# Lead-in of a fused attention and MLP kernel: one fp32 key load moved from GpSimd's queue to SyncE's, early queries first, and the last key maximum and its block scores put earlier

## The chip, the cores and the metric

One NeuronCore of one Trainium2 chip runs the whole program. The metric is device time in microseconds, as the median of several executions. TensorE (PE), VectorE (DVE), ScalarE (ACT), GpSimd (POOL) and SyncE (SP) each run their own instructions in order and wait for one another through semaphores. DMAs are started by SyncE and GpSimd, each with its own queue.

## What is computed

Inputs are q, k and v of shape (4, 8, 768, 64) and two weight matrices, 512 x 2048 and 2048 x 512, all fp32; the output is 3072 x 512 fp32. Cut to what matters:

```python
block, window = 32, 16
scale = 1.0 / np.sqrt(D)
k_sum = k.reshape(B, H, nb, block, D).max(axis=3)        # one key per block of 32: its maximum
v_sum = v.reshape(B, H, nb, block, D).mean(axis=3)
scores_l = where(|i - j| < window, scale * q @ k.T, -1e9)  # a band of near keys
scores_s = scale * q @ k_sum.T + np.log(block)             # 24 block keys
a = softmax(concat([scores_l, scores_s]))
x = a @ concat([v, v_sum])            # attention, then heads side by side
h = x @ w_in
out = (h * sigmoid(1.702 * h)) @ w_out
```

## The kernel before

Work is in bf16 and fp16 with fp32 accumulation. The four batches go one after another; the attention of the next batch is laid into the MLP of the present one, so that TensorE hardly ever stops. Only the attention of batch 0, first half (384 queries, 8 heads taken as 4 pairs of heads), has nothing to hide behind. That is the lead-in, and all of the change is in it. Weights and the rest of the inputs stream in behind it.

The order of the lead-in is written out by hand: every engine handle is a wrapper (`_Ordered`) that keeps the program order, so the list of calls in the kernel's body is the order on each engine. p counts the pairs of heads, 0 to 3.

- **Loads.** `load_k0_first` brings the fp32 keys of pair 0 by SyncE's queue to the tile k0f and `cast_k0` makes bf16 of them on ScalarE. `load_k0(p)` brings the keys of pairs 1, 2 and 3 by GpSimd's queue, which converts to bf16 on the way (tile kb). `load_q0(g)` brings the early queries of pairs 2g and 2g + 1 the same way (tile qe), `load_v0(p)` the values (tile v0n). Behind them in GpSimd's queue stand the five pieces of w_in, then w_out, late queries, w_out, the masks that GpSimd computes, and the next batch. GpSimd's DMAs use eight semaphores in turn, so each one waits for the landing of the one eight before it.
- **Keys and queries.** `k_turn(p)` transposes a pair's keys on TensorE (12 transposes into a PSUM tile ps_k), `k_own(p, engine)` copies the result to the tile qT (its second buffer). `k_max(p)` takes the maximum of each block of 32 keys on VectorE (tile ks). `q_turn(p)` and `q_copy(p, dve)` do the same for queries (PSUM tile ps_q, first buffer of qT).
- **Scores.** `s_bias(p)` writes the band's bias into PSUM (ps_s), `s_own(p)` and `s_edges(p)` add the scores, `s_exp(p)` takes the exponential on ScalarE (a_sb). `b_turn(g)` computes the block scores of two pairs into ps_b from `k_max`'s result, `b_exp(g)` their exponential (ab).
- **Values.** `v_sum` adds the value blocks on TensorE (ps_vt), `v_copy` copies them (vs). `av_own`, `av_edges` and `av_blocks` make the attention output (ps_av), `v_norm` divides it on VectorE (reciprocal rc, product x). `x_turn` and `x_copy` transpose it for the MLP (ps_x, xT), whose first matmuls (`ff_first`, then `ff_in`, PSUM tile ph) follow. The second MLP matrix goes to po.
- **Fillers.** `idle(n)` issues n matmuls on the tile warm, whose results (ps_h) nobody reads.
- **PSUM.** The lead-in's small PSUM tiles rotate through a pool of four (pturn); s_bias and the last two av_own through a pool of two (pbig).

The profile gives one line, L28 (the wrapper), to all these instructions, so steps are told apart by their tiles.

Of the kernel before, what the change touches and what calls it, by code (L numbers as in the profile page):

```python
# [9 lines left out]
F32 = mybir.dt.float32  # L10
BF16 = mybir.dt.bfloat16
# [3 lines left out]
ACT = mybir.ActivationFunctionType  # L15
# [20 lines left out]
def kernel(  # L36
# [10 lines left out]
    B, H, S, D = q.shape  # L47
# [18 lines left out]
    act = _Ordered(tc, nc.scalar)  # L66
    pool = _Ordered(tc, nc.gpsimd)
    sp = _Ordered(tc, nc.sync)
# [3 lines left out]
    castp2 = ctx.enter_context(tc.tile_pool(name="cast2", bufs=2))  # L72
# [7 lines left out]
    lead = early.enter_context(tc.tile_pool(name="lead", bufs=1))  # L80
    kb2, qb2 = {}, {}

    RK = S // 128
    RQ = 4
    PQ = HALF // RQ
    k0f = lead.tile([128, 2, RK, D], F32, name="k0f")
    qe = lead.tile([PQ, H, RQ, D], BF16, name="qe")

    def k0_rows(p):
        return k[0, 2 * p:2 * p + 2].rearrange("h (p r) d -> p h (r d)", r=RK)  # L90

    def load_k0_first():
        sp.dma_start(out=k0f.rearrange("p h r d -> p h (r d)"), in_=k0_rows(0))

    def cast_k0():
        kb2[0] = castp2.tile([128, 4, RK, D], BF16, name="kb", tag="kb")
        act.activation(out=kb2[0][:, 0:2], in_=k0f, func=ACT.Copy)

    def load_k0(p):
        if p == 2:  # L100
            kb2[1] = castp2.tile([128, 4, RK, D], BF16, name="kb", tag="kb")
        o = 2 * (p % 2)
        pool.dma_start(out=kb2[p // 2][:, o:o + 2].rearrange("p h r d -> p h (r d)"), in_=k0_rows(p))

    def load_q0(g):
        pool.dma_start(out=qe[:, 4 * g:4 * g + 4].rearrange("p h r d -> p h (r d)"),
                       in_=q[0, 4 * g:4 * g + 4, 0:HALF].rearrange("h (p r) d -> p h (r d)", r=RQ))
# [40 lines left out]
    def identity():  # L148
        pool.affine_select(out=ident, in_=ident, compare_op=ALU.not_equal, fill=1.0,
                           base=0, pattern=[[-1, 128]], channel_multiplier=1)  # L150
# [65 lines left out]
    gTb = keep.tile([128, NT, S], F16, name="gT")  # L216
# [48 lines left out]
    def copy(eng, out, in_):  # L265
        if eng is act:
            act.activation(out=out, in_=in_, func=ACT.Copy)
        elif eng == "dve_alone":

            dve.tensor_reduce(out=out, in_=in_.unsqueeze(len(in_.shape)), axis=AX.X, op=ALU.max)  # L270
        else:
            eng.tensor_copy(out=out, in_=in_)
# [21 lines left out]
    def idle(n, cols=128):  # L294

        for i in range(n):
            pe.matmul(out=st["H", 0][:, 0:cols], lhsT=warm[:, 0:128], rhs=warm[:, 0:cols],
                      start=True, stop=True)
# [70 lines left out]
    def turn_plain(ps, src):  # L369

        n, rows = src.shape[0], src.shape[2]
        for r in range(rows):
            for h in range(2):
                pe.transpose(out=ps[h * 64:h * 64 + 64, r * n:r * n + n], in_=src[:, h, r],
                             identity=ident[0:n, 0:n])
# [6 lines left out]
    def k_own(p, eng):  # L382
        copy(eng, kn[:, p].rearrange("p (c r) -> p c r", r=RK),
             st["K", p][:, 0:S].rearrange("p (r c) -> p c r", r=RK))

    def k_max(p):
        dve.tensor_reduce(out=ks0[:, p, 0:nb], in_=kn[:, p].rearrange("p (n s) -> p n s", s=block),
                          axis=AX.X, op=ALU.max)
# [8 lines left out]
    def q_turn(p):  # L397
        if p % 2 == 0:
            st["Q2"] = pturn.tile([128, 1024], BF16, name="ps_q", tag="turn")
        st["Q", p] = st["Q2"][:, p % 2 * HALF:p % 2 * HALF + HALF]  # L400
        turn_plain(st["Q", p], qe[:, 2 * p:2 * p + 2])

    def q_copy(p, eng):
        copy(eng, qT[p][0][:, 0:HALF].rearrange("p (c r) -> p c r", r=RQ),
             st["Q", p].rearrange("p (r c) -> p c r", r=RQ))
# [16 lines left out]
    def s_bias(p):  # L422

        big = st["S", p] = pbig.tile([128, 1024], F32, name="ps_s", tag="big")
        for h in range(2):
            pe.matmul(out=big[:, h * 512:h * 512 + NE], lhsT=ident, rhs=bias, start=True, stop=False,
                      skip_group_check=True)

    def s_own(p):

        big = st["S", p]
        for j in range(JH):
            for h in range(2):
                r, o = slice(h * 64, h * 64 + 64), slice(j * 128, j * 128 + 128)
                pe.matmul(out=big[:, h * 512 + j * 128:h * 512 + j * 128 + 128], lhsT=kn[r, p, o],
                          rhs=qTs[0][r, p, o], start=False, stop=True, skip_group_check=True)

    def s_edges(p):

        big = st["S", p]  # L440
        for j in range(JH):
            for h in range(2):
                r, o = slice(h * 64, h * 64 + 64), h * 512 + HALF + j * 32
                pe.matmul(out=big[0:32, o:o + 32], lhsT=kn[r, p, j * 128 + 128:j * 128 + 160],
                          rhs=qTs[0][r, p, j * 128 + 96:j * 128 + 128], start=False, stop=True,
                          skip_group_check=True)
                if j:
                    pe.matmul(out=big[96:128, o:o + 32], lhsT=kn[r, p, j * 128 - 32:j * 128],
                              rhs=qTs[0][r, p, j * 128:j * 128 + 32], start=False, stop=True,
                              skip_group_check=True)  # L450

    def s_exp(p):
        a = a_sb[p] = lead.tile([128, 2, NE], BF16, name="a_sb", tag="a_sb", bufs=4)
        act.activation(out=a, in_=st["S", p].rearrange("p (h c) -> p h c", h=2)[:, :, 0:NE],
                       func=ACT.Exp, scale=scale)

    def b_turn(g):

        st["B", g] = pturn.tile([128, 512], F32, name="ps_b", tag="turn")
        for i in range(2):  # L460
            for h in range(2):
                o = i * 64 + h * 32
                r = slice(h * 64, h * 64 + 64)
                pe.matmul(out=st["B", g][o:o + 32, 0:HALF], lhsT=ks0[r, 2 * g + i],
                          rhs=qT[2 * g + i][0][r, 0:HALF], start=True, stop=True, skip_group_check=True)

    def b_exp(g):
        ab = st["ab", g] = lead.tile([128, HALF], BF16, name="ab", tag="ab", bufs=2)
        act.activation(out=ab, in_=st["B", g][:, 0:HALF], func=ACT.Exp, scale=scale)
# [9 lines left out]
    def v_sum(ps_):  # L479

        for p in ps_:
            if p == 0:
                t = pturn.tile([128, 512], F32, name="ps_vt", tag="turn")
                st["VT", 0], st["VT", 1] = t[:, 0:2 * D], t[:, 2 * D:4 * D]
                st["VT", 0, 1] = t[:, 0:4 * D]
            elif p > 1:
                st["VT", p] = pturn.tile([128, 512], F32, name="ps_vt", tag="turn")[:, 0:2 * D]
            for i in range(2):
                for j in range(NJ):
                    o = EX - (p % 2 * 2 + i) * 32 - 4 * j  # L490
                    pe.matmul(out=st["VT", p][:, i * D:(i + 1) * D], lhsT=E[:, o:o + 128],
                              rhs=v0n[:, 2 * p + i, j, 0:D],
                              start=(j == 0), stop=(j == NJ - 1), skip_group_check=True)

    def v_copy(ps_, eng):
        h0, n = 2 * ps_[0], 2 * len(ps_)
        copy(eng, vs4[:, h0:h0 + n, 0:D], st[("VT",) + ps_].rearrange("p (h d) -> p h d", d=D))
# [383 lines left out]
    def exp_soon():  # L881
        act.activation(out=gate[:, 1:2], in_=gate[:, 0:1], func=ACT.Exp)


    dve.memset(warm, 0.0)
    dve.memset(wide, 0.0)
    load_k0_first()
    exp_soon()
    cast_k0()
    load_k0(1)  # L890
    identity()
    load_q0(0)
    load_k0(2)
    load_k0(3)
    load_q0(1)
# [24 lines left out]
    idle(4)  # L920
    k_turn(1)
    k_own(1, act)
    k_max(0)
    s_bias(1)
    idle(4)
    q_turn(0)
    q_turn(1)
    q_copy(0, dve)
    q_copy(1, dve)
    idle(8)  # L930
    s_own(0)
    s_own(1)
# [13 lines left out]
    q_copy(2, dve)  # L946
    q_copy(3, dve)
    k_max(2)
    s_bias(2)
    s_bias(3)  # L950
    v_sum((0,))
    s_own(2)
    s_own(3)
    s_edges(2)
    s_exp(2)
    s_edges(3)
    v_sum((1,))
    v_copy((0, 1), dve)
    k_max(3)
    s_exp(3)  # L960
    av_own(0)
    av_own(1)
    av_edges(0)
# [2 lines left out]
    av_blocks(1)  # L966
    v_norm(0)
    v_norm(1)
    b_turn(1)
    v_sum((2,))  # L970
    b_exp(1)
    v_copy((2,), act)
    av_own(2)
    av_edges(2)
# [29 lines left out]
    for e in range(2):  # L1004
        r = slice(64 * e, 64 * e + 64)
        dve.tensor_copy(out=w50[r, JH - e:NJ, e, :, 0:D],
                        in_=v0n[r, :, JH - e:NJ, 0:D].rearrange("p h j d -> p j h d"))
# [104 lines left out]
    for b in range(1, B - 1):  # L1112
        nxt = b + 1 < B
        s = (b + 1) % 2
# [129 lines left out]
```

## Time and profile before

| | |
|---|---|
| median of three executions | 206.87 us (206.80 to 209.70) |
| the profiled execution | 206.51 us, of which the span of the profile is 204.8 us |
| outside the span | 1.7 us |
| TensorE busy | 198.1 us, 97% of the span |
| VectorE, ScalarE, GpSimd busy | 69%, 61%, 45% of the span |
| granted TensorE clock | 0.998 over the span |
| DMA | 27.93 MB, 136 GB/s in the mean |

A busy share is no measure of what bounds the kernel. Three views answer that: the chain of waits (followed back from the last instruction to what released it), the timeline of a stretch, and the DMA issues with their time to landing. Times in them are microseconds from the span's start. A timeline row gives start, duration, engine, line, operation, output and inputs, shape and count, and in brackets the idle time before it with what ended it; DMA rows of POOL and SPq are the issuing of a DMA, not its transfer.

### The profile page before, as it was taken

To read this page: it belongs to the slowest core of one execution; us is meant where nothing else is said; L and a number is where in the kernel's file an instruction comes from. 1 tells how busy PE (TensorE), PEld (TensorE's weight loads), DVE (VectorE), ACT (ScalarE), POOL (GpSimd) and SP (SyncE) were. 2 spreads that over 40 slices of the span, in tenths; PEclk is the share of its full clock that TensorE was granted. 3 is DMA by queue.
4 is the path that set the end of the run, shared out by engine and by line. 5 is a ranking of instruction groups with operands and counts; after the bars stand their busy time and mean duration, and the time that the engine had idled before them with its cause. 6 is when DMAs were issued, how large, how long until landed. Compare 5 with 4: busy or idle time off the path is not lost.

```text
span 204.8 us, 5857 instructions
## 1 busy us (share of the span) xinstructions
PE 198.1 (97%) x2364; PEld 137.4 (67%) x2364; DVE 140.4 (69%) x388; ACT 124.6 (61%) x238; POOL 92.7 (45%) x144
## 2 busy tenths in 40 slices
PE   6989999999999999999999999999999999999992
PEld 6667654556754566665888975657888865578881
DVE  6767894594856874897768689896759546658211
ACT  4385876638786717777871546778661467983220
POOL 7965389555999584002965035000000019990000
PEclk9999999999999999999999999999999999999999
DMA  5999999999999999999999989996023730000222
GB/s 117 153 159 202 207 211 213 195 156 232 134 143 151 177 176 168 159 175 132 123 196 127 154 151 142 122 261 137 0 106 90 160 111 3 0 0 3 102 102 104
DMA packets 95851, 27.93 MB, mean 136 GB/s; under 512 B 83649, under 2 KB 92881, under 8 KB 95825
## 3 DMA queue, kind: packets, MB, share of 16 engines
q0 software_dynamic: 69920, 13.44, 85.2%
q1 hardware_dynamic: 25904, 14.13, 33.2%
q8 instruction: 18, 0.29, 0.6%
q14 instruction: 9, 0.07, 0.1%
HBM read 27.26 MB, written 6.29 MB: 164 GB/s over the span
## 4 chain that ended last, share of the span: by engine, by line
PE 90%; DMA 4%; POOL 2%; DVE 1%; issue 1%; ACT 0%; POOLq 0%; DVEq 0%
PE ph L28 33%; PE poA L28 16%; PE po L28 11%; PE poB L28 7%; PE ps_av L28 4%; DMA v0n<-in_v_dram 4%; PE poC L28 4%; PE phA L28 4%; PE ps_s L28 3%; PE ps_t L28 1%; PE ps_x L28 1%; POOL kb L28 1%; PE phB L28 1%; PE phC L28 1%; PE phE L28 1%; PE ps_vs L28 1%
## 5 line engine op out<-in xcount | busy, mean ns | idle before, releaser
L28 PE MATMUL ph<-xT,w_in_sb 128*128 128x384 f16 x416 | 70.2, 326 | 0.1
L28 PEld LDWEIGHTS <-w_in_sb 128*128 128x128 f16 x452 | 43.7, 98 | 27.8 <-issue 0.2
L28 ACT ACTIVATE gT<-ph 128x384 f16<-128x384 f32 x104 | 49.9, 492 | 18.5 <-PE ph L28 18.1
L28 PEld LDWEIGHTS <-gT 128*128 128x128 f16 x312 | 28.8, 98 | 11.3 <-issue 0.2
L28 ACT ACTIVATE a_sb<-ps_s 128x768 bf16<-128x768 f32 (+1 forms) x32 | 25.0, 826 | 12.5 <-PE ps_s L28 12.5
L28 POOL DMA_DIRECT2D vw<-in_v_dram x36 | 24.6, 700 | 12.4 <-DMA kb<-in_k_dram 4.8
L28 PEld LDWEIGHTS <-gs 128*128 128x128 f16 x288 | 27.7, 98 | 3.4
L28 POOL TENSOR_TENSOR gs<-gT 128x384 f16<-128x384 f16 x9 | 8.2, 911 | 42.3 <-ACT gT L28 42.3
L28 PE MATMUL po<-w_out_sb,gT 128*128 128x512 f16 x96 | 23.6, 380 | 0.0
L28 DVE TENSOR_TENSOR a_sb<-a_sb,mk 128x768 bf16<-128x768 bf16 x28 | 14.9, 554 | 6.5 <-ACT a_sb L28 5.9
L28 PE MATMUL poA<-ws,gs 128*128 128x256 f16 x144 | 18.7, 273 | 0.0
L28 DVE TENSOR_TENSOR x<-ps_av,rc 128x384 f16<-128x384 f32 x32 | 17.8, 558 | 1.1
L28 DVE TENSOR_TENSOR gs<-gT 128x384 f16<-128x384 f16 (+1 forms) x34 | 13.4, 394 | 7.2 <-ACT gT L28 6.9
L28 POOL DMA_DIRECT2D qb<-in_q_dram x16 | 15.1, 956 | 1.8 <-DMA w_in_sb<-in_moe_w_in_dram 1.1
L28 POOL DMA_DIRECT2D kb<-in_k_dram x15 | 14.5, 976 | 0.9 <-POOLq L1228 0.8
L28 PEld LDWEIGHTS <-kx 64*128 64x128 bf16 (+1 forms) x372 | 9.4, 95 | 6.8 <-issue 4.4
L28 DVE TENSOR_REDUCE ks<-kx 128x24 bf16<-128x768 bf16 x12 | 11.4, 949 | 3.4 <-ACT kx L28 3.2
L28 ACT ACT_TABLE_LOAD x10 | 12.8, 1283 | 1.0 <-PEq L1228 0.8
L28 ACT ACTIVATE osb<-poA 128x256 f32<-128x256 f32 x9 | 3.5, 384 | 16.0 <-PE poA L28 16.0
L28 ACT ACTIVATE s<-poA 128x256 f32<-128x256 f32 x11 | 4.2, 386 | 11.2 <-PE poA L28 11.2
L28 PEld LDWEIGHTS <-a_sb 128*64 128x64 bf16 (+2 forms) x400 | 7.8, 108 | 2.8 <-issue 1.3
L28 PE MATMUL poA<-ws,gT 128*128 128x256 f16 x72 | 9.3, 273 | 0.0
(117 smaller groups left out, 282.7 us busy)
## 6 DMA issues: line engine op xcount, KB each, us to landing
out_dram<-osb SPq DMA_DIRECT2D x23, 256.0 KB, 3.3
kb<-in_k_dram POOLq DMA_DIRECT2D x15, 192.0 KB, 7.1
qb<-in_q_dram POOLq DMA_DIRECT2D x12, 192.0 KB, 10.9
vw<-in_v_dram POOLq DMA_DIRECT2D x36, 64.0 KB, 5.7
w_out_sb<-in_moe_w_out_dram POOLq DMA_DIRECT2D x4, 512.0 KB, 13.0
w_in_sb<-in_moe_w_in_dram POOLq DMA_DIRECT2D x3, 512.0 KB, 12.9
vw<-vs SPq DMA_DIRECT2D x6, 198.0 KB, 6.1
v0n<-in_v_dram POOLq DMA_DIRECT2D x4, 192.0 KB, 8.1
```

The lines of the kernel that those rows point to most:

```text
L28: r = f(*a, **kw)
```

## The change

- The keys of pair 1 go as fp32 by SyncE's queue, right behind those of pair 0, and are cast on ScalarE by a second activation, which stands ahead of `k_own(0)` on that engine. The two fp32 buffers are no longer a tile of their own: they lie in a part of gT (the MLP's activations), which is written only later.
- GpSimd's first DMA is therefore the early queries of pairs 0 and 1 (before: the keys of pair 1), ahead of `identity()`. Its queue has one DMA less.
- On TensorE `q_turn(0)` and `q_turn(1)` come right behind `k_turn(1)`, ahead of `s_bias(1)`, and four of the filler matmuls are gone. On VectorE `k_max(0)` goes from ahead of the first two `q_copy` to behind them.
- On VectorE `k_max(3)` goes from behind `v_copy((0, 1))` to right behind `k_max(2)`.
- On TensorE `b_turn(1)` goes from behind `av_blocks(1)` to between `v_sum((0,))` and `v_sum((1,))`; `v_sum((0,))` goes from ahead of `s_own(2)` to behind `s_edges(3)`. On ScalarE the order stays: `s_exp(2)`, `s_exp(3)`, `b_exp(1)`.

```diff
-    k0f = lead.tile([128, 2, RK, D], F32, name="k0f")
+    k0f = {}
...
-    def load_k0_first():
-        sp.dma_start(out=k0f.rearrange("p h r d -> p h (r d)"), in_=k0_rows(0))
-
-    def cast_k0():
-        kb2[0] = castp2.tile([128, 4, RK, D], BF16, name="kb", tag="kb")
-        act.activation(out=kb2[0][:, 0:2], in_=k0f, func=ACT.Copy)
+    def load_k0_first(p):
+
+        k0f[p] = gTb.rearrange("p t s -> p (t s)").bitcast(F32)[:, (4 + p) * 2 * RK * D:(5 + p) * 2 * RK * D] \
+            .rearrange("p (h c) -> p h c", h=2)
+        sp.dma_start(out=k0f[p], in_=k0_rows(p))
+
+    def cast_k0(p):
+        if p == 0:
+            kb2[0] = castp2.tile([128, 4, RK, D], BF16, name="kb", tag="kb")
+        act.activation(out=kb2[0][:, 2 * p:2 * p + 2].rearrange("p h r d -> p h (r d)"), in_=k0f[p], func=ACT.Copy)
...
-    load_k0_first()
+    for p in range(2):
+        load_k0_first(p)
     exp_soon()
-    cast_k0()
-    load_k0(1)
+    for p in range(2):
+        cast_k0(p)
+    load_q0(0)
     identity()
-    load_q0(0)
     load_k0(2)
...
     k_turn(1)
     k_own(1, act)
-    k_max(0)
-    s_bias(1)
-    idle(4)
     q_turn(0)
     q_turn(1)
+    s_bias(1)
     q_copy(0, dve)
     q_copy(1, dve)
+    k_max(0)
     idle(8)
...
     k_max(2)
+    k_max(3)
     s_bias(2)
     s_bias(3)
-    v_sum((0,))
     s_own(2)
     s_own(3)
     s_edges(2)
     s_exp(2)
     s_edges(3)
+    s_exp(3)
+    v_sum((0,))
+    b_turn(1)
+    b_exp(1)
     v_sum((1,))
     v_copy((0, 1), dve)
-    k_max(3)
-    s_exp(3)
     av_own(0)
...
     v_norm(1)
-    b_turn(1)
     v_sum((2,))
-    b_exp(1)
     v_copy((2,), act)
```

## The prediction

> **What bounds the kernel now.** I read the chain of waits first, by engine and then in order of time for the first 60 us. The columns of the second fence are start, length and what held the chain.
>
> ```profile
> PE 90%; DMA 4%; POOL 2%; DVE 1%; issue 1%; ACT 0%; POOLq 0%; DVEq 0%
> ```
>
> ```profile
> 6.34 8.11 DMA v0n<-in_v_dram
> ...
> 14.49 0.53 PE ps_vt L28 x12
> 15.02 1.30 PE ps_av L28 x38
> 16.32 0.41 PE ps_b L28 x4
> 16.73 0.47 PE ps_vt L28 x12
> ...
> 20.45 10.07 PE ph L28 x62
> ```
>
> TensorE carries 90% of the chain. The only long piece that is not TensorE's is the second value load (v_sum(1) starts at 14.49, when it lands). From 20.45 on matmuls follow without a gap. So the change can only move the moment at which that dense part begins, and what is won or lost ahead of it comes out in the time one for one, as long as the weights are there. I therefore went through the timeline of the first 17 us; here is the part up to the first scores.
>
> ```profile
> 0.82 0.44 SPq L28 DMA_DIRECT2D k0f<-in_k_dram  x1
> ...
> 1.32 0.87 POOL L28 DMA_DIRECT2D kb<-in_k_dram  x1 [0.80 <-POOLq L1228]
> ...
> 3.88 0.84 ACT L28 ACTIVATE kb<-k0f 128x768 bf16<-128x768 f32 x1 [1.56 <-DMA k0f<-in_k_dram]
> ...
> 5.66 0.81 ACT L28 ACTIVATE qT<-ps_k 128x768 bf16<-128x768 bf16 x1 [0.94 <-PE ps_k L28]
> ...
> 6.51 0.95 DVE L28 TENSOR_REDUCE ks<-qT 128x24 bf16<-128x768 bf16 x1
> ...
> 6.58 0.53 PE L28 MATMUL ps_k<-wide,kb 128*64 128x128 bf16 x12
> 7.03 0.58 PE L28 MATMUL ps_s<-bias,wide 128*128 128x480 bf16 x2
> ...
> 7.45 0.39 PE L28 MATMUL ps_h<-warm 128*128 128x128 bf16 x4
> ...
> 7.84 0.53 PE L28 MATMUL ps_q<-wide,qe 96*64 96x96 bf16 x16
> ...
> 8.31 0.62 PE L28 MATMUL ps_h<-warm 128*128 128x128 bf16 x8
> 8.42 1.02 DVE L28 COPY qT<-ps_q 128x384 bf16<-128x384 bf16 x2 [0.96 <-PE ps_q L28]
> ...
> 9.36 0.94 DVE L28 TENSOR_REDUCE ks<-qT 128x24 bf16<-128x768 bf16 x1
> ```
>
> The early queries are transposed at 7.84 because they land then. Call the start of q_turn(0) x: before, x = 7.84. The DMA issues, each asked for alone, give the landings.
>
> ```profile
> k0f<-in_k_dram SPq DMA_DIRECT2D x1, 384.0 KB, 3.0
> kb<-in_k_dram POOLq DMA_DIRECT2D x1, 192.0 KB, 5.0
> ```
>
> ```profile
> qe<-in_q_dram POOLq DMA_DIRECT2D x1, 192.0 KB, 5.3
> ```
>
> Pair 0's keys land at 0.82 + 3.0 = 3.82, GpSimd's first DMA (pair 1's keys) at 1.32 + 5.0 = 6.32. The queries, 5.3 after their issue, land at 7.83.
>
> **Step 1: the fp32 keys of pair 1.** While only SyncE's transfer ran (2.2 to 3.0 us), the DMA view shows its speed:
>
> ```profile
> DMA packets 180, 0.28 MB, mean 346 GB/s; under 512 B 0, under 2 KB 180, under 8 KB 180
> ```
>
> 384 KB, 0.39 MB, at 346 GB/s is 1.13 us. Right behind the first, the second lands at 4.95 if it has the engines to itself, and at 6.1 if the queries take turns with it. The second cast, 0.84, ends between 5.8 and 6.95. k_turn(1) starts at 6.58 for TensorE's own order (bias and fillers ahead of it), so the early end costs nothing and the late end 0.4. I take the early end, since SyncE issues its second DMA at about 1.26 (0.82 + 0.44), before GpSimd's first issue ends at 2.19. On ScalarE k_own(0) now waits behind the second cast: from 5.66 to at most 6.95. Its reader is s_own(0), which comes at 8.5 by the steps below, so it is covered by 0.7 us.
>
> **Step 2: the queries first.** The queries take the slot whose DMA landed at 6.32. They now have two SyncE transfers beside them instead of one: between nothing and 1.13 us more, so 6.32 to 7.45. TensorE is not there before the end of k_turn(1), at 7.03 (the row that followed it). So x lies between 7.03 and 7.45; I take 7.05, 0.8 earlier than before. The nearest row is the first DMA's own 5.0 us, in which one SyncE transfer already ran until 3.82, and the second would be over by 4.95, 1.4 us ahead of that landing.
>
> The Trainium skill, page "DMA: Bandwidth & Descriptors", section "Queues, rings and completion order", says that each DMA engine takes turns, packet by packet, between the queues that have work for it. Behind the row of 346 GB/s with one queue alone, it speaks for the end at 7.45; the trace of before has two queues together only in the last tenths of the first transfer, so it does not settle it. By that rule the queries come 0.4 later than I take, and this is the first rival.
>
> **Step 3: what follows x on TensorE and VectorE.** These rows give the distances.
>
> ```profile
> 10.01 0.53 PE L28 MATMUL ps_k<-wide,kb 128*64 128x128 bf16 x12
> ...
> 10.47 0.34 PE L28 MATMUL ps_b<-qT,ks 64*32 64x384 bf16 x4
> 10.58 0.96 DVE L28 COPY qT<-ps_k 128x768 bf16<-128x768 bf16 x1 [0.28 <-PE ps_k L28]
> ...
> 11.32 0.53 PE L28 MATMUL ps_q<-wide,qe 96*64 96x96 bf16 x16
> ...
> 11.89 1.02 DVE L28 COPY qT<-ps_q 128x384 bf16<-128x384 bf16 x2 [0.36 <-PE ps_q L28]
> ...
> 13.12 0.76 PE L28 MATMUL ps_s<-qT,qT 64*128 64x128 bf16 x32
> ...
> 15.39 0.94 DVE L28 TENSOR_REDUCE ks<-qT 128x24 bf16<-128x768 bf16 x1
> ...
> 16.25 0.48 PE L28 MATMUL ps_b<-qT,ks 64*32 64x384 bf16 x4
> ...
> 16.66 0.54 PE L28 MATMUL ps_vt<-v0n,E 128*128 128x64 bf16 x12
> ```
>
> The two query copies run from x + 0.58 to x + 1.60 (8.42 and 9.44 against 7.84). TensorE meanwhile has q_turn 0.47 (7.84 to 8.31), the bias 0.42 (7.03 to 7.45) and eight fillers 0.6, so s_own(0) starts at x + 1.5. The four fillers taken out cost nothing to miss: they filled 0.39 us of a wait.
>
> On VectorE k_max(0), which ran from 6.51 in an idle stretch, now stands behind the query copies. That is the price of this order: k_max(0) and k_max(1) follow each other, 0.94 each, each starting 0.08 before the one ahead ends (9.36 against 9.44), and end at x + 3.32. Three things wait for that. k_own(2) starts at x + 3.3 (before 10.58; with x = 7.05 that is 10.35). On TensorE b_turn(0) needs both maxima, and k_turn(3) and q_turn(2), q_turn(3) are queued behind it: k_turn(3) at x + 3.5, plus 0.46 (10.01 to 10.47) gives q_turn(2) at x + 4.0. The next two query copies start 0.57 later (11.32 to 11.89), at x + 4.55, and end at x + 5.57. k_max(2) starts at x + 5.49, k_max(3) 0.86 after it, and ends at x + 7.3.
>
> On TensorE s_own(2) to s_edges(3), 0.76, and v_sum(0), some 0.5, are done by x + 6.6, where the copies above let them start. Then b_turn(1) stands and waits for k_max(3), with v_sum(1) and everything after it queued behind. Before, 0.33 us lay between the end of k_max(3) (15.39 + 0.94 = 16.33) and the next TensorE step (16.66). So v_sum(1) starts at x + 7.63 = 14.68, a little later than its 14.49 before: the wait for values has become a wait for VectorE.
>
> From v_sum(1) to v_sum(2) it was 16.66 - 14.49 = 2.17 us, of which b_turn(1) took 0.41 (chain row at 16.32). Without it 1.76 are left. v_sum(2) starts at x + 9.39 = 16.44 instead of 16.66. The sum: 16.66 - 9.39 - x = **7.27 - x**, which is 0.22 us earlier at x = 7.05, nothing at 7.27, and 0.57 later at 7.84. All that follows on the three engines is in the old order and keeps its distances; b_exp(1) comes earlier on ScalarE and leaves v_copy(2) no later.
>
> **Step 4: the streams behind.** GpSimd's queue has one DMA less. The slot between the first landing and the second was 7.83 - 6.32 = 1.51 us; SyncE's transfer that replaces it takes 1.13 of the same engines, so all later loads come 0.38 to 1.5 us earlier. v_sum(1)'s values then land by 14.1, ahead of 14.68. The tightest weight is the first piece of w_out:
>
> ```profile
> 14.73 0.74 POOL L28 DMA_DIRECT2D w_out_sb<-in_moe_w_out_dram  x1 [1.10 <-DMA v0n<-in_v_dram]
> ```
>
> ```profile
> w_out_sb<-in_moe_w_out_dram POOLq DMA_DIRECT2D x1, 512.0 KB, 15.4
> ```
>
> ```profile
> 30.36 1.89 PE L28 MATMUL po<-w_out_sb,gT 128*128 128x512 f16 x8
> ```
>
> It lands at 14.73 + 15.4 = 30.13 for a use at 30.36, only 0.23 ahead. With the loads 0.38 earlier at least and TensorE 0.22 earlier the cover holds; if the loads came no earlier, it would still just hold.
>
> **The rivals.** *First, on the slower side: the early queries come late.* If SyncE's second transfer holds them up so that they land after 7.27, the order that puts k_max(0) behind the copies costs more than b_turn(1) saves. At 7.45 the cost is 7.45 - 7.27 = 0.18, at 7.84, as late as before, 0.57. The time is then 207.05 to 207.45. For it speaks that the second transfer doubles what runs beside the queries; against it that pair 0's transfer did not keep GpSimd's first DMA from landing at 6.32.
>
> *Second, a larger gain: VectorE's chain is not what b_turn(1) waits for.* Should k_max(3) end by x + 6.6, v_sum(1) starts when TensorE is free, 13.65, or when its values land, at most 14.1. v_sum(2) then starts at 15.4 to 15.9, a gain of 0.8 to 1.25 and a time of 205.6 to 206.1. For it speaks that the values do land earlier; against it that seven VectorE instructions in a row have to shrink by 0.7 us.
>
> *Third, it does not do what it says:* k_max(3) and the block scores do come about two microseconds sooner, but TensorE waits for them and the time is the same within 0.1 us: 206.8 to 206.95, the middle between forecast and first rival. I count it to these.
>
> **The numbers.** The sum is made on the execution of 206.51 us (span 204.8): 206.3 afterwards, span 204.6. The median of the runs is 0.36 higher, so 206.87 - 0.22 gives 206.65, rounded 206.6. Chances: forecast (0.05 to 0.5 earlier) 0.48, first rival 0.36, second 0.12, and 0.04 for something that the profile does not show. The range runs from the middle of the second rival, 205.8, to the far end of the first, 207.45, plus the scatter of the three runs near their median: 208.1. I call 2%, 4.1 us, about what a measurement of this kernel can tell from no change. The whole stretch that is touched has a wait or two of 0.6 us each to give, so no case reaches that: faster 0.01, within 0.97, slower 0.02 (one of the three runs before was 1.4% higher).
>
> **What would show it.** Right: q_turn(0) near 7.05; the second cast over by 6.6; on TensorE a wait for ks of 0.5 to 0.9 us ahead of b_turn(1), and none for v0n; v_sum(1) at 14.7 and v_sum(2) at 16.4; the long row of ph some 0.2 earlier. Wrong: q_turn(0) waiting for qe (first rival), no wait ahead of b_turn(1) (second), or a wait for weights in the first MLP.

## The result and the profile after

| | before | after |
|---|---|---|
| median of 22 executions | 207.94 us | 206.66 us |
| lowest and highest | 206.80 to 210.04 | 205.33 to 208.07 |
| ratio after to before | | 0.9939, 95% interval 0.9917 to 0.9961 |
| profiled execution (span) | 206.51 (204.8) | 207.68 (205.9) |

The change gains 0.6%, 0.8 to 1.7 us by the interval. Ratios, here and below, leave out the few slow executions, which took over 1.5% more than the fastest of their kernel. The forecast, 206.6, is met, but by luck: it was made against 206.87. With more executions the kernel before has 207.94, and the gain, 1.28 us, is some six times the 0.22 us of the sum. The two profiled executions seem to say the opposite of the medians: that of after is 1.1 us longer in its span. That has to be cleared up first.

The chain of waits of after, first by engine, then pieces of it in order of time:

```profile
PE 89%; DMA 5%; DVE 3%; ACT 1%; issue 0%; SPq 0%; DVEq 0%
```

```profile
0.82 3.22 DMA gT<-in_k_dram
...
12.79 1.02 DVE qT L28 x2
13.81 1.73 DVE ks L28 x2
...
15.59 0.34 PE ps_b L28 x2
15.92 0.47 PE ps_vt L28 x12
16.39 1.30 PE ps_av L28 x38
17.70 0.36 PE ps_vt L28 x12
...
21.32 10.08 PE ph L28 x62
```

The 8.11 us of v0n are gone. In their place stand the query copies, k_max(2) and k_max(3) on VectorE, and then b_turn(1): the chain that step 3 named. But the long row of ph starts at 21.32, not earlier than the 20.45 of before. The timeline of after shows why:

```profile
5.09 0.84 ACT L28 ACTIVATE kb<-gT 128x768 bf16<-128x768 f32 x1 [0.18 <-DMA gT<-in_k_dram]
...
7.08 0.85 PE L28 MATMUL ps_k<-wide,kb 128*64 128x128 bf16 x12
...
7.72 0.85 PE L28 MATMUL ps_q<-wide,qe 96*64 96x96 bf16 x16
...
8.51 0.98 PE L28 MATMUL ps_s<-bias,wide 128*128 128x480 bf16 x2
...
9.28 1.06 PE L28 MATMUL ps_h<-warm 128*128 128x128 bf16 x8
...
11.15 0.53 PE L28 MATMUL ps_k<-wide,kb 128*64 128x128 bf16 x12
...
15.59 0.34 PE L28 MATMUL ps_b<-qT,ks 64*32 64x384 bf16 x2 [0.39 <-DVE ks L28]
15.86 0.54 PE L28 MATMUL ps_vt<-v0n,E 128*128 128x64 bf16 x12
```

The same twelve key transposes take 0.85 us at 7.08 and 0.53 at 11.15, eight fillers 1.06 instead of 0.62, the query transposes 0.85 instead of 0.53. TensorE ran at half speed until some moment between; the trace's record of the granted clock has the rise at 10.7 us in this execution and at 6.2 us in the profiled one of before. The two profiles can't be subtracted from each other.

The Trainium skill, page "TensorE: Matmul & The Clock Gate", Part 1, says that TensorE starts at half clock and that busy time releases it, judged in windows of 3413 ns which run freely and do not begin with the kernel. The traces agree in part. TensorE always starts at 1.3 us, and in twelve of the 14 profiles of this case the rise lies between 4.4 and 6.7, a spread of less than one such window. The two profiles of the changed kernel, with 10.7 and 10.8, lie more than a window behind all others, and no run here shows why.

### The profile page after: what moved, and what is told of

It reads as the page before. It is cut to its first block, busy times and chain, and to the rows that moved or that the text cites. A ratio compares the mean times of both kernels' runs of the same rounds, so it can differ in the third digit from the quotient of the medians.

```text
span 205.9 us, 5854 instructions
## 1 busy us (share of the span) xinstructions
PE 199.3 (97%) x2360; PEld 138.5 (67%) x2360; DVE 140.8 (68%) x388; ACT 125.2 (61%) x239; POOL 92.1 (45%) x143
## 4 chain that ended last, share of the span: by engine, by line
PE 89%; DMA 5%; DVE 3%; ACT 1%; issue 0%; SPq 0%; DVEq 0%
PE ph L28 33%; PE poA L28 16%; PE poB L28 8%; PE po L28 8%; PE ps_av L28 4%; PE poC L28 4%; PE phA L28 4%; PE ps_s L28 4%; DMA vw<-vs 3%; DMA gT<-in_k_dram 2%; PE ps_x L28 1%; PE ps_k L28 1%; PE ps_t L28 1%; PE phB L28 1%; PE phC L28 1%; PE ps_q L28 1%
## 5 line engine op out<-in xcount | busy, mean ns | idle before, releaser
L28 DVE TENSOR_TENSOR gs<-gT 128x384 f16<-128x384 f16 (+1 forms) x34 | 13.3, 393 | 6.9 <-ACT gT L28 6.6
L28 POOL DMA_DIRECT2D kb<-in_k_dram x14 | 13.6, 985 | 0.3 <-issue 0.3
L28 PE MATMUL poA<-w_out_sb,gT 128*128 128x256 f16 x72 | 9.4, 273 | 0.0
```

Of the source, the lines that this page charges most:

```text
L28: r = f(*a, **kw)
```

## The experiments

Each kernel was timed against the kernel before on the same chip. An edit is one of the kernel before or of the changed kernel, as said, and is cut to the moved calls ("..." stands for lines left out).

**The loads alone.** The kernel before with only this, and the two functions as the change has them:

```diff
...
-    load_k0_first()
+    for p in range(2):
+        load_k0_first(p)
     exp_soon()
-    cast_k0()
-    load_k0(1)
+    for p in range(2):
+        cast_k0(p)
+    load_q0(0)
     identity()
-    load_q0(0)
```

> Only the loads of the change (pair 1's keys as fp32 by SyncE, queries first on GpSimd), all orders on TensorE, VectorE and ScalarE as before. Theory L (the loads): the whole stream behind comes some 1.4 us earlier, and in most executions of the kernel before TensorE waits for it, though not in the profiled one of 206.51, which is faster than nearly all others. Then the loads alone give the whole gain, 1.1 to 1.5 us, ratio near 0.994. Theory C (the prediction's chain): only the begin of the first MLP matmuls counts; the early queries are worth 0.3 to 1.0 us where TensorE's clock rises early and nothing where it rises late, in the mean 0.4 us, ratio 0.998.

Measured: ratio 0.9979 (0.9944 to 1.0014). The interval holds the value of theory C (0.998); theory L's 0.994 lies just outside it. In its profile, with the clock up at 4.5 us, the queries landed at 6.67 and were transposed only at 8.20, behind key transposes that waited for the second cast, the bias and the fillers:

```profile
7.01 0.53 PE L28 MATMUL ps_k<-wide,kb 128*64 128x128 bf16 x12 [0.70 <-ACT kb L28]
7.47 0.58 PE L28 MATMUL ps_s<-bias,wide 128*128 128x480 bf16 x2
7.88 0.39 PE L28 MATMUL ps_h<-warm 128*128 128x128 bf16 x4
8.20 0.53 PE L28 MATMUL ps_q<-wide,qe 96*64 96x96 bf16 x16
...
13.87 0.50 PE L28 MATMUL ps_vt<-v0n,E 128*128 128x64 bf16 x11
15.03 0.19 PE L28 MATMUL ps_vt<-v0n,E 128*128 128x64 bf16 x1 [0.65 <-issue]
```

So earlier queries were worth nothing in this execution. The order on TensorE was one reason. The second profile of the kernel before shows it as well: there the queries landed at 2.53 + 4.3 = 6.83 and were transposed at 7.91, when the bias and four fillers were done. Two things besides held this execution back: the second cast came late, and v_sum(1), which began 0.6 us earlier than before, stopped for 0.65 us ahead of its last matmul, with no engine or DMA that the profile names as the cause. Such halts come again below. The rows of the second profile of before:

```profile
qe<-in_q_dram POOLq DMA_DIRECT2D x1, 192.0 KB, 4.3
```

```profile
7.17 0.58 PE L28 MATMUL ps_s<-bias,wide 128*128 128x480 bf16 x2
7.59 0.39 PE L28 MATMUL ps_h<-warm 128*128 128x128 bf16 x4
7.91 0.53 PE L28 MATMUL ps_q<-wide,qe 96*64 96x96 bf16 x16
```

**The orders alone.** The kernel before with the front and back orders of the change:

```diff
-    k_max(0)
-    s_bias(1)
-    idle(4)
     q_turn(0)
     q_turn(1)
+    s_bias(1)
     q_copy(0, dve)
     q_copy(1, dve)
+    k_max(0)
...
     k_max(2)
+    k_max(3)
...
+    v_sum((0,))
+    b_turn(1)
+    b_exp(1)
     v_sum((1,))
```

> Only the orders of the change on TensorE and VectorE (front and back), all loads as before. Theory L: no change, ratio 1.000, or slightly slower. Theory C: the wait of b_turn(1) for the last key maximum without earlier queries, 0.4 to 0.6 us slower, ratio 1.002 to 1.003. A third possibility, that the orders themselves give the gain: ratio 0.994 to 0.996.

Measured: ratio 1.0007 (0.9979 to 1.0035). That the orders by themselves give the gain (0.994 to 0.996) is out. The forecast wait is there, 0.39 us for ks ahead of b_turn(1)'s second half at 15.54; the loss in time is within what the comparison can tell.

**The back part undone in the changed kernel.**

```diff
     k_max(2)
-    k_max(3)
...
-    v_sum((0,))
-    b_turn(1)
-    b_exp(1)
     v_sum((1,))
     v_copy((0, 1), dve)
+    k_max(3)
...
     v_norm(1)
+    b_turn(1)
     v_sum((2,))
+    b_exp(1)
```

> The changed kernel with k_max(3), b_turn(1), v_sum(0) and b_exp(1) back in their old places. Theory L: as the changed kernel, ratio 0.994. Theory C: the wait of b_turn(1) for the key maximum goes, values are there in time: 0.5 us faster than the changed kernel, ratio near 0.991 if the changed kernel has 0.994.

Measured: ratio 0.9953 (0.9927 to 0.9980). Nearly the whole gain is there without the back part, but not more than with it; theory C's 0.991 is out. The profile (clock up at 4.4 us) shows what stood in the place of the wait that went:

```profile
6.42 0.53 PE L28 MATMUL ps_q<-wide,qe 96*64 96x96 bf16 x16
...
12.82 0.54 PE L28 MATMUL ps_vt<-v0n,E 128*128 128x64 bf16 x12
13.20 0.26 PE L28 MATMUL ps_av<-v0n,a_sb 128*128 128x65 bf16 x3
14.25 0.91 PE L28 MATMUL ps_av<-v0n,a_sb 128*128 128x65 bf16 x29 [0.80 <-issue]
```

v_sum(1) ran at 12.82, 1.7 us earlier than before, and then TensorE stood still for 0.80 us in the middle of av_own, with no engine or DMA that the profile could name as the cause.

**The back part alone**, in the kernel before (the reverse of the diff above).

> The kernel before with only the back part of the change (k_max(3) behind k_max(2), b_turn(1) ahead of v_sum(1), v_sum(0) behind s_edges(3)). Theory L: no change, ratio 1.000. Theory C: 0.1 to 0.6 us slower, ratio 1.001 to 1.003, and a wait for ks ahead of b_turn(1). If the back part makes the gain: ratio below 0.997.

Measured: ratio 1.0014 (0.9984 to 1.0044), with 0.40 us of waiting for ks ahead of b_turn(1). The sign is theory C's, but the interval holds no change as well; the back part gives no clear gain by itself.

**The changed kernel once more.**

> The changed kernel once more, beside the other three on one chip. Theory P (position of the clock's rise): the first profile of the changed kernel had TensorE's clock full only from 10.7 us on, that of the kernel before from 6.2 on, so the two profiles can't be compared; in an execution with an early rise the first long row of ph starts at 19.7 to 20.0 instead of 21.3, and b_turn(1) still waits 0.4 to 0.7 us for ks. Theory L (the loads bound the MLP): the start of ph is the same in both and the gain is found behind 30 us. Ratio near 0.994 by both.

Measured: ratio 0.9971 (0.9937 to 1.0004), a weaker gain than in the first comparison; the two intervals overlap between 0.9937 and 0.9961. Its profile (208.74 us) is again one with a late rise, at 10.8 us, so it could not show the early case. It shows a second source of scatter, far behind the lead-in. The view of who waited for whom, TensorE from 21 us on:

```profile
PE ps_av L28 <- DMA vw<-vs: 1.1, 1, 1.1
```

There batch 1's value sums wait for a transfer within the chip. The same wait was 0.3 us in the first profile of after and absent in the first of before; in the profile of the loads alone 1.0 us was lost at another place, at 142 us, to a wait for VectorE. From the first matmul of the MLP to the end the 14 profiles need between 185.1 and 186.6 us, though the work is the same.

**b_turn(1) late.** The changed kernel with the early k_max(3), but b_turn(1) and b_exp(1) back in their old places:

```diff
-    b_turn(1)
-    b_exp(1)
     v_sum((1,))
...
     v_norm(1)
+    b_turn(1)
     v_sum((2,))
+    b_exp(1)
```

> The changed kernel with b_turn(1) and b_exp(1) back behind av_blocks(1); k_max(3) stays early. Theory P and the prediction's chain: the wait for ks ahead of v_sum(1) goes, 0.4 us earlier than the changed kernel at the first matmuls of the MLP at the same position of the clock's rise; ratio to before 0.992 if all of it reaches the end. Rival: the wait was harmless because v_sum(1) or the next instructions wait for something else; then ratio as the changed kernel, 0.994, and another wait in its place.

Measured: ratio 0.9968 (0.9937 to 0.9999), as the changed kernel beside it. The rival holds: the wait for ks went, and the halt without a named cause came back, now 1.04 us, at the same matmul, the fourth of av_own:

```profile
15.04 0.91 PE L28 MATMUL ps_av<-v0n,a_sb 128*128 128x65 bf16 x29 [1.04 <-issue]
```

**k_max(0) ahead of the query copies** in the changed kernel:

```diff
     k_own(1, act)
+    k_max(0)
     q_turn(0)
...
     q_copy(1, dve)
-    k_max(0)
```

> The changed kernel with k_max(0) back ahead of the first two query copies on VectorE. The prediction's step 3 says that k_max(0) behind the copies delays k_max(3) and so b_turn(1): 0.3 to 0.4 us earlier than the changed kernel where the clock rises early, nothing where it rises late, because TensorE is then the bound. Ratio 0.992 to 0.994. Rival: k_max(0) ahead holds up the copies (the second cast delays k_own(0) on ScalarE): 0.2 us slower than the changed kernel, ratio 0.995.

Measured: ratio 0.9938 (0.9918 to 0.9959). In the direction of step 3, though the intervals of this kernel and of the changed one beside it overlap. Both sides of the expectation are in its profile: k_max(0) waited for k_own(0) until 7.59 and the copies started 1.19 us behind q_turn(0) instead of 0.58, and yet v_sum(1) came at x + 7.48 (14.75, x = 7.27). Here, too, TensorE then stopped ahead of v_sum(1)'s last matmul, for 0.26 us.

**The kernel before against itself.**

> The kernel before against itself, for the scatter and a second profile. Ratio 1.000; what its interval reaches is what these comparisons can tell. Theory P: another position of the clock's rise and with it another start of the MLP (20.3 to 21.0). Theory L: a wait for weights in the first MLP, which the first profile lacks.

Measured: ratio 0.9994 (0.9963 to 1.0025); differences below 0.3% can't be told in such a comparison. No wait for weights, theory L's sign, appeared. The profile (209.26 us) holds the most instructive execution of the kernel before:

```profile
15.45 0.52 PE L28 MATMUL ps_vt<-v0n,E 128*128 128x64 bf16 x12 [1.48 <-DMA v0n<-in_v_dram]
```

```profile
16.90:20.20 3.30, 3.30 (x49) 2.58 (x48) 1.98 (x6) 0.77 (x2) 1.74 (x3) 0.50 1.29 206
20.40:22.00 1.60, 1.53 (x34) 1.23 (x30) 0.90 (x3) 0.99 (x3) 0.70 (x1) 1.00 1.24 207
```

The second fence gives busy time by stretch; in each row the third number from the end is the granted clock. v_sum(1) waited 1.48 us for values, not 0.61, and behind that wait the clock was 0.50 for 3.4 us (16.8 to 20.2 by its record). From v_sum(1) to the first matmul of ph it took 6.37 us (15.45 to 21.82) against 5.15 in the first profile (14.49 to 19.64): the fall cost 1.2 us. The same page of the Trainium skill puts the return to half clock after an idle window of about 3.4 us; here the clock fell behind a wait of 1.48 us, and the measurement decides.

**One load more.** The changed kernel with pair 1's keys loaded a second time, to a tile that nobody reads, so that the stream behind stands as before the change:

```diff
     identity()
+    spare_k = lead.tile([128, 2, RK, D], BF16, name="spare_k")
+    pool.dma_start(out=spare_k.rearrange("p h r d -> p h (r d)"), in_=k0_rows(1))
     load_k0(2)
```

> The changed kernel plus one load that nobody reads: pair 1's keys once more on GpSimd's queue, behind the first queries, so that everything behind stands where it stood before the change. Theory V (the values): the kernel before waits in most executions longer for the second pair's values than its first profile showed (landing at 14.4 to 15.4), the changed one never (12.5 to 13.3); that is where the gain comes from. Then the landing goes back to 14 to 15.4, v_sum(1) waits for v0n again and the ratio to before goes up to 0.998 to 1.001. Rival O (the early queries and the orders give it): ratio stays at 0.994 to 0.997.

Measured: ratio 0.9946 (0.9923 to 0.9968); seven executions. The values landed at 14.62, as late as before, and the gain stayed. Theory V falls: ratio and landing are those of rival O, and v_sum(1), at 14.68, came just behind its values. This profile is also the fair partner of the first one of before, because its clock rose at 6.1 us:

```profile
6.93 0.51 PE L28 MATMUL ps_q<-wide,qe 96*64 96x96 bf16 x16
...
14.34 0.34 PE L28 MATMUL ps_b<-qT,ks 64*32 64x384 bf16 x2 [0.40 <-DVE ks L28]
14.68 0.52 PE L28 MATMUL ps_vt<-v0n,E 128*128 128x64 bf16 x12
...
16.34 0.53 PE L28 MATMUL ps_vt<-v0n,E 128*128 128x64 bf16 x12
```

**Fillers in the wait for values**, in the kernel before (they write a spare part of the PSUM tile ps_vt):

```diff
+                st["VT", 0, 2] = t[:, 4 * D:4 * D + 128]
...
     s_edges(3)
+    for i in range(12):
+        pe.matmul(out=st["VT", 0, 2], lhsT=warm[:, 0:128], rhs=warm[:, 0:128], start=True, stop=True,
+                  skip_group_check=True)
     v_sum((1,))
```

> The kernel before with twelve filler matmuls, read by nobody, between s_edges(3) and v_sum(1), where it waits for values. In its second profile TensorE's clock fell to half for 3.4 us behind a wait of 1.5 us there, and the stretch to the MLP took 1.2 us longer. If such falls weigh in the mean: no execution with a mean clock of 0.992 or less, ratio 0.997 to 0.999. If they are too rare: ratio 1.000, slowest executions gone. If the fillers come too late for the values: up to 0.2 us slower.

Measured: ratio 1.0011 (0.9990 to 1.0033). No execution of the twelve had a mean clock below 0.996, and the slowest took 208.5 us, against 211.2 for the kernel before beside it, three of whose 24 executions had 0.984 to 0.992. No fall of the clock is seen, as the second expectation has it: they are too rare to move the middle. But the fillers have a price of their own in this kernel's profile, which can hide a small gain. The transposes of x that follow the first ph began 1.00 us behind it (0.46 to 0.48 in the other 13 profiles), though their weights were loaded at 20.48:

```profile
20.00 0.48 PE L28 MATMUL ph<-xT,w_in_sb 128*128 128x384 f16 x2
21.00 0.33 PE L28 MATMUL ps_x<-ident,x 128*128 128x128 f16 x3 [0.51 <-DVE x L28]
```

**Both costs undone.** The changed kernel with k_max(0) ahead of the copies and b_turn(1) late (the two diffs above together).

> The changed kernel with both undone that cost it something: k_max(0) ahead of the query copies, b_turn(1) and b_exp(1) behind av_blocks(1). By the chain the first long row of ph starts 0.3 to 0.7 us earlier than in the changed kernel at the same position of the clock's rise: ratio 0.991 to 0.993. Rival: other waits take their place (TensorE's instruction supply, which showed a stall of 0.8 to 1.0 us in av_own in two profiles, or later transfers): ratio as the changed kernel, 0.994 to 0.997.

Measured: ratio 1.0012 (0.9978 to 1.0046), the gain lost, outside both forecasts. Seven of twelve executions had a mean clock of 0.981 to 0.992. The profile:

```profile
13.54 0.26 PE L28 MATMUL ps_av<-v0n,a_sb 128*128 128x65 bf16 x3
15.82 1.29 PE L28 MATMUL ps_av<-v0n,a_sb 128*128 128x65 bf16 x29 [2.03 <-issue]
```

```profile
16.10:22.80 6.70, 6.70 (x106) 5.61 (x104) 2.44 (x8) 1.54 (x4) 2.90 (x4) 0.50 1.27 206
```

```profile
q8 instruction: 1, 0.02, 5.9%
```

The halt is 2.03 us here, again at the fourth matmul of av_own, and behind it TensorE ran at half clock for 6.8 us. The last fence, from the DMA view of 13.2 to 14.4 us, has a transfer of instructions (one packet of 16,384 bytes, from 13.26 to 14.39) beside DMA engines busy with the inputs.

The traces say more about these halts than the single profiles do. Counted in the matmul records, all five lie ahead of TensorE's 224th matmul, whatever it is: the last of v_sum(1) in the kernels with the loads alone and with k_max(0) early, the fourth of av_own in the other three. In each such a transfer (1.1 us) runs ahead of it, and TensorE goes on 1.34 to 1.57 us behind the transfer's end. In none of the other nine profiles does the 224th matmul start less than 1.39 us behind that end; in the first profile of before it is 1.49, so that an earlier v_sum(1) would probably have met the same halt. The transposes of x in the kernel with fillers begin with the 352nd matmul, 128 further on, 1.41 us behind the end of the next transfer.

**The same with 32 fillers at the start.**

```diff
-    idle(28)
+    idle(32)
```

> The same with 32 fillers at the start instead of 28, which close the gap of 0.3 to 0.5 us ahead of the first key transposes. If the gap is what lets the clock's rise slip to 10.7 us (two profiles of the changed kernel): the slow executions get rarer, median 0.2 to 0.5 us under the kernel with 28. If not: no difference, or 0.1 us slower where the keys land early.

Measured: ratio 0.9917 (0.9892 to 0.9942), six executions, median 206.31: the lowest ratio of all kernels tried, 0.8% under the kernel before. Four matmuls more at the start, and TensorE no longer stops:

```profile
13.71 0.52 PE L28 MATMUL ps_vt<-v0n,E 128*128 128x64 bf16 x12 [0.57 <-DMA v0n<-in_v_dram]
14.07 1.01 PE L28 MATMUL ps_av<-v0n,a_sb 128*128 128x65 bf16 x32
```

The 224th matmul is another one now, the last of v_sum(1), the transfer ran from 10.9 us on instead of 13.3, and v_sum(1) waits 0.57 us for its values again. Why the transfer ran earlier is not shown, nor whether the moved place or the earlier transfer ended the halt. The expectation was about the clock's early rise, and this run does not tell that (it rose at 5.8 us with 28 fillers and at 5.7 with 32).

## Why the prediction was right, and where it was short

Starts of the early queries' transposes (x) and of the MLP's first matmul, in us, with the moment from which the clock was full:

| kernel | clock full | x | first ph | span |
|---|---|---|---|---|
| before, first profile | 6.2 | 7.84 | 19.64 | 204.8 |
| before, second profile | 6.6, half from 16.8 to 20.2 | 7.91 | 21.82 | 207.6 |
| after, first profile | 10.7 | 7.72 | 20.50 | 205.9 |
| after, second profile | 10.8 | 8.21 | 20.79 | 207.0 |
| after, one load more | 6.1 | 6.93 | 19.31 | 204.4 |
| after, back part undone | 4.4 | 6.42 | 18.80 | 204.6 |
| both costs undone, 32 fillers | 5.7 | 6.75 | 18.72 | 204.7 |

- **Step 1, second key load.** In the first profile of after it landed at 5.04 and the cast ran from 5.09 to 5.93, as taken; in the second it landed at 6.64, past the late end of the bounds (6.1), and k_turn(1) waited for it until 7.57.
- **Step 2 and the first rival.** Which of the two came true changes from one execution to the next. The DMA view of after, from 3 to 4 us, has SyncE's queue alone, and the queries landed at 1.38 + 5.5 = 6.88:

```profile
q1 hardware_dynamic: 276, 0.40, 106.5%
```

  By the rule of the page "DMA: Bandwidth & Descriptors", section "Queues, rings and completion order", of the Trainium skill the two queues would take turns. In the first profile the second transfer had the engines nearly to itself, since GpSimd's first packets came only at 4.25. They came at 4.1 to 4.3 us in all nine profiles with the new loads and at 3.0 to 3.3 in the five with the old; whether SyncE's second transfer or the other first load makes the difference is not isolated. In the second profile of after its packets lasted beyond 5 us beside the queries', and those landed at 7.28. There x was 8.21, later than before, but not by the first rival's path: the keys were late, not the queries. k_turn(1) had waited 0.64 us for the second cast:

```profile
7.57 0.85 PE L28 MATMUL ps_k<-wide,kb 128*64 128x128 bf16 x12 [0.64 <-ACT kb L28]
```
- **Step 3, the formula.** It holds. With one load more and x = 6.93 it gives v_sum(1) at 14.56 and v_sum(2) at 16.32; measured 14.68 and 16.34. The wait for ks ahead of b_turn(1) is 0.4 us (forecast 0.5 to 0.9), and there is none for v0n. Against the first profile of before, at the same position of the clock's rise, first ph is 0.33 us earlier and the span 0.4; the formula says 7.27 - 6.93 = 0.34. In the late executions it is 0.5 us short (15.86 against 15.35 at x = 7.72), because the clock is at half for three of its links.
- **The terms that were mis-sized** are x and the base. I took 7.03 as TensorE's own limit, from one execution in which part of the way to it ran at half clock; with the clock up at 4.4 us x is 6.42 (back part undone), where the formula gives 0.85 us of gain. And I moved the whole difference onto the median by a constant 0.36 us, as if the median were the profiled execution plus scatter. The profiled one of before was faster than all 22 timed ones: a second one waited 0.9 us more for values and lost 1.2 us of clock. So the agreement of 206.6 with 206.66 is luck: the base was 1.07 us too low and the gain 1.06 us too small. The gain lies outside the 0.05 to 0.5 of the forecast. Nor is the range worked out at its upper end: its last 0.65 us, called scatter, come from no row.
- **What q_turn(0) waited for before.** The landing at 7.83 was not all. The bias and four fillers ahead of it end at about 7.76 (estimate: 7.45 and four fillers of 78 ns), so an earlier landing alone could win less than 0.1 us there. With the orders alone TensorE is there first and waits 0.15 us for qe (q_turn(0) at 7.53). That would explain why neither part does much without the other.
- **The second rival** (VectorE's chain no longer waited for) forecast a gain of 0.8 to 1.25 us, near the measured one, but its condition did not come about: in both profiles of the changed kernel b_turn(1) waits for ks. Where it was forced, by taking b_turn(1) away from there, TensorE ran early into the halt. So the wait that I charged to the change was cheap: it stood in front of another. The third rival, the same time within 0.1 us, is out by the interval.
- **Step 4.** The loads came earlier by about the upper bound of 1.5 us: w_out's first piece landed at 28.57 and 29.05 in the two profiles of after, 30.13 and 30.59 in those of before. No wait for weights appeared. With one load more it landed at 30.32 and the gain stayed, so this did not decide.

**What stays open.** Clear gains have only kernels with the loads and the front order together: the change itself (0.994; its second comparison, 0.997, reaches 1.000), with its back part undone (0.995), with k_max(0) early (0.994), with one load more (0.995), with both costs undone and 32 fillers (0.992), and barely with b_turn(1) late (0.997). Both costs undone with 28 fillers (1.001) lost the gain to the halt. Either part alone shows nothing clear (0.998 and 1.001), though the halt also took 0.65 us from the loads alone in their profile. That the early start of the query transposes carries the gain agrees with all of them, but it is argued and not isolated. It makes 0.3 to 0.9 us by the formula, with nothing in a late execution, and the first comparison measured 0.8 to 1.7. The rarer falls of the clock add little: 9 of the 94 executions of the kernel before that these experiments were compared with had a mean clock of 0.992 or less, 1 of 34 of the changed one, and at 1.2 us each that is 0.1 us in the mean. How often the clock rises early or late in either kernel, and how often each one halts at its 224th matmul, would be needed for the rest, and the profiles are too few to say.

## What to carry to other kernels

A sum of a few tenths from one profile is only as good as that execution: look first at what differs between executions (here the moment at which the clock rises, and landings that scatter by 1 us), and compare profiles at equal positions of it. Where a load is moved forward, see whether the engine that consumes it can come to it earlier; here neither move did anything clear alone. Before a wait is taken away, see what stands behind it: three kernels here ran into a halt that the wait had covered.

## What the runs showed of the hardware

- TensorE's halts without a named cause lie at one fixed count in its program, its 224th matmul (0.26, 0.65, 0.80, 1.04 and 2.03 us in five kernels), with a 16,384-byte instruction transfer that ended 1.34 to 1.57 us ahead of the restart. 128 matmuls, each with its weight load, are 256 instructions. That the instructions came late is the reading that fits all 14 profiles; no run delayed such a transfer by itself, and that DMA engines full with inputs delay it is only likely. The Trainium skill, page "Runtime: NRT & Kernel Launch", section "Instruction fetch mechanics", has refills in blocks of 16 KiB (256 instructions) and calls their cost mostly hidden. The size agrees with the trace; hidden they are not here.
- Behind a wait of 1.48 us and one of 2.03 us on TensorE, in the midst of dense work, its clock was half for 3.4 and for 6.8 us. A halt of 1.04 us had no such fall behind it.
- The clock shown for a stretch is 1.00 also before its first recorded rise, while the rows tell of half speed (28 fillers of 113 ns each there, against 78 ns for eight later). Row lengths tell it, not that column.
